# Two of six low parts a head from PSUM on VectorE, and the operand splits moved to GpSimd and ScalarE

## The chip, the cores and the metric

The kernel runs on one core of one Trainium2 chip. The metric is the device time of one execution in microseconds. A core has a tensor engine (PE, with its weight loads as PEld), a vector engine (DVE), a scalar engine (ACT), a GpSimd engine (POOL), and a sync engine (SP) that issues the transfers. The first three reach PSUM; GpSimd and the transfers work on SBUF.

## The reference

The inputs are q, k and v of 4 batches x 8 heads x 768 tokens x 64 columns. Queries and keys are given the nearest of 16 centroids of their head, and a query sees only the keys of its own cluster:

```python
q_assign = np.argmax(np.einsum('bhsd,hcd->bhsc', q_n, c_n), axis=-1)
k_assign = np.argmax(np.einsum('bhsd,hcd->bhsc', k_n, c_n), axis=-1)
mask = q_assign[:, :, :, None] == k_assign[:, :, None, :]
scores = np.where(mask, scale * np.matmul(q, k.transpose(0, 1, 3, 2)), -1e9)
scores = scores - np.max(scores, axis=-1, keepdims=True)
attn = np.exp(scores)
attn = attn / (np.sum(attn, axis=-1, keepdims=True) + 1e-09)
x = np.matmul(attn, v)          # then [3072, 512]: heads side by side
# soft mixture of experts on x: 8 experts, 4 slots each, 512 -> 1024 -> 512
logits = x @ phi
d = softmax(logits, axis=0); slot_input = d.T @ x
h = np.maximum(slot_input[e] @ w1[e], 0.0); slot_out[e] = h @ w2[e]
out = softmax(logits, axis=1) @ slot_out
```

The two softmax lines are shortened; all else is as in the reference.

## The kernel before

**What is done for a head.** There are 32 heads (a head here is one of 4 x 8), handled in pairs. Matrix products keep near float32 precision by splitting operands into a high and a low part. For each head `load_r` brings q and k, transposed, as one tile of 128 rows x 768 columns. `split_hi` rounds it (L512), `split_lo` takes the rest (L515), and ten small transfers (`place1`, `place2`, `place_mask`, `place3`, L325) lay the parts out as the operands of the score passes. For each pair, VectorE finds the cluster of each token (`assign1` to `assign3`, L473 to L488), and the mask goes into the operands too. V is split likewise into float16 parts (`splitv_hi`, L543, and `splitv_lo`, L547).

`pass_a` (L560) makes the scores of a head in nine steps of one PSUM bank each, with two banks in turn, and VectorE takes the row maxima of each step (`rowmax`, L568). The maxima are transposed and placed as one more operand row. `pass_b` (L603) then makes the scores again, less the maxima, with 128 keys on the partitions and 768 queries in the columns: six tiles a head, in two PSUM buffers `pb` in turn, an even tile in the first and an odd one in the second. ScalarE takes the exponential of a tile twice (`expo`, L609), once to float32 and once to float16, both in SBUF. The float16 copy is the high part; `elow` (L613) subtracts it from the float32 copy, on GpSimd, and writes the low part. `pass_c` (L625) multiplies both parts with the parts of v, two tiles at a time, and `norm` (L637 to L639) divides by the row sums.

**After the heads** the logits of each pair are added up, each batch of eight heads is routed, and at the end the experts' two layers run on 32 slots and the result is combined for all tokens (from L1022). Expert weights come in 16 chunks of 2 MB, five of them during the attention, the others into the buffers that the attention gives back.

**What sets the order.** Every step is recorded as an operation with an engine, an assumed duration and the buffers that it reads and writes. `Plan.order` goes through them with a clock of its own: each engine takes, of the operations that can start now or within the waiting time of their kind, the one with the lowest priority. Priorities are the numbers of the table `K`. The result is one fixed sequence for each engine, and on the chip an engine works through its sequence strictly in order, waiting on semaphores. The planner before assumes 0.23 us from one engine to another and knows nothing of one engine slowing another. `HI_ACT` is true for the heads 0 and 1 only, so from head 2 on both splits of q and k and both of v are VectorE's, while GpSimd does nothing but the six subtractions a head (in the last head two of six).

Of the kernel before, what the change touches and what calls it, by code (L numbers as in the profile page):

```python
# [21 lines left out]
HI_ACT = lambda i: i < 2 or i % 2 == HA  # L22
HA = 2
MX_ACT = False
WARM0 = 60
WARM1 = (0, 4, 3, 2, 4, 1)   # after the last xtrans, xtrans, logits, dtrans, slotin, comb
EARLY = 2              # heads whose first steps keep off the vector engine


class Plan:  # L30
    """Operations in program order, with the buffers that they read and write; order() lets every
    engine take, of the operations that can start or do so soon, the one of the lowest priority number."""

# [13 lines left out]
    def op(self, eng, us, key, t, fn, rd=(), wr=(), get=None, put=None, after=(), xfer=0.0):  # L47
# [16 lines left out]
        self.ops.append((eng, us, t + self.K[key], fn, deps, get, put, xfer, key, t))  # L64
# [12 lines left out]
    def order(self, look=LOOK, banks=1):  # L77
        N = len(self.ops)
        users = [[] for _ in range(N)]
        wait = [len(o[4]) for o in self.ops]  # L80
        for n, o in enumerate(self.ops):
            for d in o[4]:
                users[d].append(n)
        ready = [0.0] * N
        end = [None] * N
        free, cand, out = {}, {}, []
        dma = tail = 0.0
        gets, puts = [], {}

        def opened(n):  # L90
            cand.setdefault(self.ops[n][0], []).append(n)

        def start(n):
            t = ready[n]
            if self.ops[n][5] is not None and len(gets) >= banks:
                p = puts.get(gets[-banks])
                if p is None:
                    return None
                t = max(t, p + self.LAT)
            return t  # L100

        for n in range(N):
            if wait[n] == 0:
                opened(n)
        while len(out) < N:
            best = None
            for e, ns in cand.items():
                f = free.get(e, 0.0)
                ts = [(max(f, s), n) for s, n in ((start(n), n) for n in ns) if s is not None]
                if not ts:  # L110
                    continue
                t0 = min(ts)[0]
                if best is None or t0 < best[0]:
                    best = (t0, e, ts)
            t0, e, ts = best
            _, _, t, n = min((self.ops[n][2], n, t, n) for t, n in ts
                             if t <= t0 + self.K.get(self.ops[n][8] + "_wt", look))
# [14 lines left out]
            if get is not None:  # L132
                gets.append(get)
# [1099 lines left out]
```

## Time and profile before

| | |
|---|---|
| three runs | 564.26, 564.88, 568.58 us |
| median | 564.88 us |
| span of the profiled execution, first to last instruction | 563.4 us |
| busy: PE, DVE, ACT, POOL | 478.6, 465.5, 340.2, 345.7 us |
| normalisation of head 0, head 3, head 27, head 31 begins | 49.08, 107.45, 458.86, 498.95 us |

The profiled execution has no time of its own beside its span; the span is 0.9 us under the fastest of the three runs and 1.5 us under their median. The run has three stretches. Up to about 107 us the first heads fill the pipeline. From there to about 459 us the heads follow one another evenly. Then the last four heads run without preparation of further ones, and from about 499 us the experts follow.

A busy time includes what an instruction waits once it has started. On PE it also includes the modelled end of pipelined products, so that PE is never quite as busy as its figure. Two instructions that follow each other directly on VectorE overlap by about 0.08 us in the records.

### The profile page before, as it was taken

To read this page: it belongs to the slowest core of one execution; us is meant where nothing else is said; L and a number is where in the kernel's file an instruction comes from. 1 tells how busy PE (TensorE), PEld (TensorE's weight loads), DVE (VectorE), ACT (ScalarE), POOL (GpSimd) and SP (SyncE) were. 2 spreads that over 40 slices of the span, in tenths; PEclk is the share of its full clock that TensorE was granted. 3 is DMA by queue.
4 is the path that set the end of the run, shared out by engine and by line. 5 is a ranking of instruction groups with operands and counts; after the bars stand their busy time and mean duration, and the time that the engine had idled before them with its cause. 6 is when DMAs were issued, how large, how long until landed. Compare 5 with 4: busy or idle time off the path is not lost.

```text
span 563.4 us, 15227 instructions
## 1 busy us (share of the span) xinstructions
PE 478.6 (85%) x6083; PEld 376.8 (67%) x6083; DVE 465.5 (83%) x786; ACT 340.2 (60%) x494; POOL 345.7 (61%) x255
## 2 busy tenths in 40 slices
PE   8896868789888889789888889887988799899994
PEld 6685657577767667667676667776765678764484
DVE  3799698998989998989899998999899988452253
ACT  4176536676667667667676667676765687830142
POOL 7067465777767657777766578676866598714210
PEclk9999878999999999999999999999999899999998
DMA  8824537346656566676666646665765478999978
GB/s 222 216 70 120 152 98 204 102 130 186 172 142 178 147 154 164 178 177 155 169 168 180 155 125 161 181 176 151 174 175 151 132 204 203 308 311 382 408 248 239
DMA packets 55082, 103.79 MB, mean 184 GB/s; under 512 B 8490, under 2 KB 22372, under 8 KB 55012
## 3 DMA queue, kind: packets, MB, share of 16 engines
q1 hardware_dynamic: 55012, 102.82, 65.2%
q8 instruction: 48, 0.79, 0.6%
q14 instruction: 22, 0.18, 0.1%
HBM read 52.76 MB, written 6.29 MB: 105 GB/s over the span
## 4 chain that ended last, share of the span: by engine, by line
DVE 49%; PE 28%; DMA 12%; issue 5%; SPq 3%; ACT 1%; POOL 0%; DVEq 0%; ACTq 0%; POOLq 0%
DVE mc L568 16%; DMA w<-w 11%; DVE w L515 8%; PE pa L560 6%; PE pc L625 6%; DVE vx L543 5%; PE pb L603 5%; DVE w L512 3%; PE pso L1103 3%; PE ph L1041 2%; SPq L325 2%; DVE w L478 2%; DVE w L488 2%; DVE vx L547 2%; PE po L1124 2%
## 5 line engine op out<-in xcount | busy, mean ns | idle before, releaser
L613 POOL TENSOR_TENSOR w<-w,w 128x768 f16<-128x768 f32 x188 | 322.6, 1737 | 161.1 <-PE pc L625 81.7
L609 ACT ACTIVATE w<-pb 128x768 f32<-128x768 f32 (+1 forms) x384 | 285.0, 815 | 105.0 <-PE pb L603 102.5
L568 DVE TENSOR_REDUCE mc<-pa 128x1 f32<-128x512 f32 (+1 forms) x288 | 187.4, 679 | 17.9 <-PE pa L560 16.7
L560 PE MATMUL pa<-w 128*128 128x512 f32 (+1 forms) x384 | 120.9, 386 | 56.3 <-DVE mc L568 44.1
L603 PE MATMUL pb<-w 128*128 128x512 f32 (+1 forms) x576 | 152.6, 353 | 1.5 <-DMA w<-w 1.4
L625 PE MATMUL pc<-vx,w 128*128 128x65 f16 (+1 forms) x3456 | 123.0, 194 | 3.3 <-DVE w L639 3.0
L560 PEld LDWEIGHTS pa<-w 128*128 128x128 f32 x384 | 61.4, 191 | 89.0 <-DVE mc L568 72.4
L625 PEld LDWEIGHTS <-w 128*128 128x128 f16 x3456 | 112.3, 98 | 11.3 <-DVE w L639 3.9
L603 PEld LDWEIGHTS pb<-w 128*128 128x128 f32 x576 | 105.0, 193 | 18.2 <-issue 1.7
L603 PE MATMUL pb<-w,w 128*128 128x512 f32 x192 | 61.0, 340 | 0.0
L515 DVE TENSOR_TENSOR w<-w,w 128x768 fp32r<-128x768 f32 x30 | 48.9, 1630 | 0.1
L603 PEld LDWEIGHTS pb<-w,w 128*128 128x128 f32 x192 | 36.5, 190 | 7.1 <-DVE w L592 0.3
L543 DVE TENSOR_SCALAR vx<-w 128x384 f16<-128x384 f32 x30 | 35.6, 1185 | 0.0
L512 DVE CAST w<-w 128x768 fp32r<-128x768 f32 x30 | 27.6, 919 | 3.5 <-DMA w<-w 2.8
L462 ACT ACTIVATE w<-pt,crn 128x384 f32<-128x384 f32 x16 | 9.3, 581 | 30.7 <-PE pt L454 30.6
L547 DVE SCALAR_TENSOR_TENSOR vx<-w,vx 128x384 f16<-128x384 f32 x32 | 25.5, 797 | 1.8 <-ACT vx L541 1.7
L992 PE MATMUL pc<-ident 128*128 128x128 f32 x148 | 22.0, 301 | 1.4 <-POOL ident masks.py:199 1.4
L992 PEld LDWEIGHTS pc<-ident 128*128 128x128 f32 x148 | 20.2, 212 | 3.1 <-issue 1.6
L500 ACT ACTIVATE w<-pt,ohsc 128x768 fp32r<-128x768 bf16 x15 | 13.5, 901 | 12.5 <-PE pt L497 12.4
L653 ACT COPY xT<-pt 128x384 f32<-128x384 f32 x30 | 14.6, 488 | 10.0 <-PE pt L648 10.0
L488 DVE TENSOR_TENSOR w<-w,m 128x192 bf16<-128x192 bf16 x32 | 19.4, 645 | 0.3
L478 DVE TENSOR_TENSOR w<-w,descb 128x384 bf16<-128x384 bf16 x16 | 19.0, 1190 | 0.0
(138 smaller groups left out, 379.3 us busy)
## 6 DMA issues: line engine op xcount, KB each, us to landing
w<-w SPq DMA_DIRECT2D x128, 192.0 KB
w<-w SPq DMA_DIRECT2D x188, 96.0 KB
w<-w1r SPq DMA_DIRECT2D x64, 256.0 KB
w<-qkT SPq DMA_DIRECT2D x32, 384.0 KB
w<-w2a SPq DMA_DIRECT2D x32, 256.0 KB
w<-w2b SPq DMA_DIRECT2D x16, 512.0 KB
w<-vt SPq DMA_DIRECT2D x32, 192.0 KB
out<-w SPq DMA_DIRECT2D x24, 256.0 KB
```

Source lines behind the costliest of these rows:

```text
L488: nc.vector.tensor_tensor(oh[:, :, k, 0:NCL], wv[:, :, k, :], mv[:, :, k].unsqueeze(2).to_broadcast([P, NG // 2, NCL]), op=cmp)
L512: (nc.scalar.copy if HI_ACT(i) else nc.vector.tensor_copy)(RH[i % 2], R[i % 3])
L515: (nc.gpsimd if i < EARLY else nc.vector).tensor_sub(RL[i % 2], R[i % 3], RH[i % 2].bitcast(F32))
L543: nc.vector.tensor_scalar_mul(o, V[i % 2], VS)
L547: nc.vector.scalar_tensor_tensor(vx[:, :, 0:D], V[i % 2], VS, vx[:, :, D:2 * D], op0=ALU.mult, op1=ALU.subtract)
L560: nc.tensor.matmul(pa[:, c0:c0 + w], q1[:, q0:q0 + P], k1[:, k0:k0 + w], start=True, stop=True)
L568: nc.vector.tensor_reduce(hd[i]["mc"][:, 4 * m + c0:4 * m + c1], pa.rearrange("p (n c) -> p n c", n=c1 - c0), axis=AX.X, op=ALU.max, negat ...
L603: nc.tensor.matmul(pbt[j % 2][:, q0:q1], k_[:, kc], q_[:, q0:q1], start=(o == 0), stop=(o == 1))
L609: nc.scalar.activation(dst[:, j % 2, :], pbt[j % 2][:, 0:S], AF.Exp, scale=SCALE)
L613: eng.tensor_tensor(EL[(NT * i + j) % NEL], E32[o % 2][:, j % 2, :], EH[o % (NEH // 2)][:, j % 2, :], op=ALU.subtract)
L625: nc.tensor.matmul(pc[:, t * W:t * W + w], e[:, ts], vx[:, j, r0:r0 + w], start=(j == 0 and t == 0 and o == 0), stop=(j == NT - 1 and o == ...
L992: nc.tensor.matmul(d["pc"][:, 0:P], ident, ident, start=True, stop=True)
```

## The change

**Exponentials.** Of the six tiles of a head, the tiles 1 and 3 (`'PDPDPP'`; in the last head 1, 3 and 5) are handled in a new way. ScalarE still takes the exponential twice, now the float16 one first, and the float32 one is written over the scores in the `pb` buffer. VectorE subtracts from there (L607 of the changed kernel), and `pb` is free for the next scores only when it is done. The other four tiles are subtracted on GpSimd as before. The four float32 buffers in SBUF are now handed out to GpSimd's tiles alone, one by one.

**Splits.** From head 2 on, `split_hi` is ScalarE's in even heads and GpSimd's in odd ones, `split_lo` and `splitv_hi` are GpSimd's, and `splitv_lo` stays on VectorE. The heads 0 and 1 are as before.

**Constants.** The small constants of the last stage (`consts3`, `consts4`) are made at the start instead of in pair 1.

**Planner.** It lets an operation that it marks with `port`, and every operation of GpSimd, run only when no other such one does. Its latencies now differ by engine, transfers take longer in it, many durations are new, and the whole table `K` is new. The expert stage is the same.

```diff
-HI_ACT = lambda i: i < 2 or i % 2 == HA
-HA = 2
-MX_ACT = False
+SPLITS = (('ACT', 'POOL', 'POOL', 'DVE'), ('POOL', 'POOL', 'POOL', 'DVE'))
+EARLY_SPLITS = ("ACT", "POOL", "ACT", "DVE")
+LOWS = ('PDPDPP', 'PDPDPP')
+LAST_LOWS = "PDPDPD"
...
-    LAT = 0.23            # from one engine to another
-    DMA_ISSUE, DMA_DONE = 0.65, 1.0
+    LAT = {"PE": 0.22, "ACT": 0.22, "DVE": 0.14, "POOL": 0.14, "-": 0.0}
+    SAME = {"DVE": 0.11}
+    DMA_ISSUE, DMA_DONE = 1.25, 2.4
...
+            if o[10]:
+                t = max(t, port)
+            return max(t, free[o[0]])
...
+            if lock:
+                port = end
...
-    E32 = [cols(ar5, n * 2 * S, 2 * S).rearrange("p (t s) -> p t s", t=2) for n in range(2)]
+    NE32 = 4
+    E32 = [cols(ar5, n * S, S) for n in range(NE32)]
...
-        b3=-150.8, b4=97.0, b5=70.0, x=387.35, el=-51.8, c0=-14.95, c1=102.4, c2=224.45, c3=204.0,
+        maxrow_out=-367.85, b0=955.45, b1=175, b2=-738.8, b3=626.95, b4=-23.65, b5=335.4, x=322.8, el=-141.85,
...
+    ENG = dict(ACT=nc.scalar, DVE=nc.vector, POOL=nc.gpsimd)
+
+    def splits(i):
+        return EARLY_SPLITS if i < EARLY else SPLITS[i % 2]
+
+    def lows(i):
+        return LAST_LOWS if i == NH - 1 else LOWS[i % 2]
+
     def split_hi(i):
-        (nc.scalar.copy if HI_ACT(i) else nc.vector.tensor_copy)(RH[i % 2], R[i % 3])
+        e = splits(i)[0]
+        (nc.scalar.copy if e == "ACT" else ENG[e].tensor_copy)(RH[i % 2], R[i % 3])
 
     def split_lo(i):
-        (nc.gpsimd if i < EARLY else nc.vector).tensor_sub(RL[i % 2], R[i % 3], RH[i % 2].bitcast(F32))
+        ENG[splits(i)[1]].tensor_sub(RL[i % 2], R[i % 3], RH[i % 2].bitcast(F32))
...
     def splitv_hi(i):
-        o = VXs[i % 2][:, :, D:2 * D]
-        if i < EARLY:
-            nc.scalar.mul(o, V[i % 2], VS)
-        else:
-            nc.vector.tensor_scalar_mul(o, V[i % 2], VS)
+        e = splits(i)[2]
+        (nc.scalar.mul if e == "ACT" else ENG[e].tensor_scalar_mul)(VXs[i % 2][:, :, D:2 * D], V[i % 2], VS)
...
+    def e32(i, j):
+        if lows(i)[j] == "D":
+            return pbt[j % 2][:, 0:S]
+        return E32[e32n[NT * i + j] % NE32]
+
     def expo(i, j):
-        o = (NT * i + j) // 2
-        for dst in (E32[o % 2], EH[o % (NEH // 2)]):
-            nc.scalar.activation(dst[:, j % 2, :], pbt[j % 2][:, 0:S], AF.Exp, scale=SCALE)
-
-    def elow(i, j, eng):
-        o = (NT * i + j) // 2
-        eng.tensor_tensor(EL[(NT * i + j) % NEL], E32[o % 2][:, j % 2, :], EH[o % (NEH // 2)][:, j % 2, :],
-                          op=ALU.subtract)
+        n = NT * i + j
+        for dst in (EH[n // 2 % (NEH // 2)][:, j % 2, :], e32(i, j)):
+            nc.scalar.activation(dst, pbt[j % 2][:, 0:S], AF.Exp, scale=SCALE)
+
+    def elow(i, j):
+        n = NT * i + j
+        (nc.vector if lows(i)[j] == "D" else nc.gpsimd).tensor_tensor(
+            EL[n % NEL], e32(i, j), EH[n // 2 % (NEH // 2)][:, j % 2, :], op=ALU.subtract)
...
+    op("POOL", 0.6, "const1", 0, consts3, [], [("const", 3)])
+    op("DVE", 1.1, "const1", 0, consts4, [], [("const", 4)])
...
+                if lows(i)[j] == "D":
+                    op("ACT", 1.385, "x", t, lambda i=i, j=j: expo(i, j), [("pb", n)], [("eh", n), ("pb", n)])
+                    op("DVE", 0.88, "el", t, lambda i=i, j=j: elow(i, j), [("pb", n), ("eh", n)], [("el", n)])
```

**The order on VectorE**, in the evenly running stretch, behind the division of a head's result (`w_98` is the result, `w_97` a row of maxima or a part of an exponential, `w_88` and `w_89` the tile of q and k and its parts, `w_96` the tile of v, `vx` its parts, `pa` and `pb` the score banks). Before:

```order
L639 TENSOR_TENSOR w_98<-pc,z 128x2x3x64
L583 CAST w_97<-pt 6x128
L568 TENSOR_REDUCE mc<-pa_134 128x2
L568 TENSOR_REDUCE mc<-pa_133 128x1
L512 CAST w_89<-w_88 128x768
L543 TENSOR_SCALAR vx_121<-w_96 128x6x64
L568 TENSOR_REDUCE mc<-pa_134 128x1
L568 TENSOR_REDUCE mc<-pa_133 128x1
L515 TENSOR_TENSOR w_89<-w_88,w_89 128x768
```

and now, from the transfer of the maxima on:

```order
L571 CAST w_97<-pt 6x128
L535 SCALAR_TENSOR_TENSOR vx_121<-w_96,vx_121 128x6x64
L556 TENSOR_REDUCE mc<-pa_133 128x1
L607 TENSOR_TENSOR w_97<-pb_132,w_97 128x768
L556 TENSOR_REDUCE mc<-pa_133 128x1
L556 TENSOR_REDUCE mc<-pa_134 128x2
L453 TENSOR_REDUCE mx<-pt 128x24
L454 TENSOR_TENSOR w_88<-pt,mx 128x384
```

The three splits between the row maxima are gone, and a subtraction from the second score buffer (`pb_132`) stands there instead. A little later in the same pair the next one stands behind the products of the assignment:

```order
L556 TENSOR_REDUCE mc<-pa_134 128x2
L458 TENSOR_TENSOR w_88<-w_88,descb 128x384
L463 TENSOR_REDUCE m_3236<-w_88 128x24
L607 TENSOR_TENSOR w_97<-pb_132,w_97 128x768
L556 TENSOR_REDUCE mc<-pa_133 128x1
```

From here on the program repeats itself pair by pair: 41 instructions of VectorE, four of them subtractions, of which the other two stand right behind a row maximum.

**The order on GpSimd.** Before, 173 subtractions follow one another with nothing between them:

```order
L515 TENSOR_TENSOR w_89<-w_88,w_89 128x768 x2
L613 TENSOR_TENSOR w_97<-w_96,w_97 128x768 x15
L219 MEMSET grp 128x4
L221 MEMSET grp 32x1 x4
L613 TENSOR_TENSOR w_97<-w_96,w_97 128x768 x173
```

and now one pair of heads reads:

```order
L506 TENSOR_TENSOR w_89<-w_88,w_89 128x768
L607 TENSOR_TENSOR w_97<-w_96,w_97 128x768 x3
L531 TENSOR_SCALAR vx_121<-w_96 128x6x64
L607 TENSOR_TENSOR w_97<-w_96,w_97 128x768 x2
L503 CAST w_89<-w_88 128x768
```

The splits stand between subtractions that wait for ScalarE and for free buffers, and behind them on the queue.

## Rows read from the trace of the kernel before

**Rows 1.** Page, part 1: busy time, share of the span, instructions of each engine.

```profile
PE 478.6 (85%) x6083; PEld 376.8 (67%) x6083; DVE 465.5 (83%) x786; ACT 340.2 (60%) x494; POOL 345.7 (61%) x255
```

**Rows 2.** Windows: us, busy (count) of PE, PEld, DVE, ACT, POOL; PEclk, DMA.

```profile
100.00:400.00 300.00, 254.78 (x3338) 204.73 (x3337) 279.22 (x462) 204.29 (x293) 211.70 (x123) 1.00 0.61 159
```

**Rows 3.** Timeline (start us, us): divisions of heads 0, 3, 27, 31.

```profile
49.08 0.56 DVE L639 TENSOR_TENSOR w<-pc,z 128x384 f32<-128x384 f32 x1
...
107.45 0.56 DVE L639 TENSOR_TENSOR w<-pc,z 128x384 f32<-128x384 f32 x1
...
458.86 0.56 DVE L639 TENSOR_TENSOR w<-pc,z 128x384 f32<-128x384 f32 x1
...
498.95 0.36 DVE L639 TENSOR_TENSOR w<-pc,z 128x192 f32<-128x192 f32 x1
```

**Rows 4.** Waits from 100 to 400 us: us in total, times, longest us.

```profile
ACT w L609 <- PE pb L603: 68.7, 67, 2.4
...
POOL w L613 <- PE pc L625: 58.4, 29, 3.9
...
PE pa L560 <- DVE mc L568: 27.0, 34, 1.5
```

**Rows 5.** Page, part 4: the chain that ended last, by engine.

```profile
DVE 49%; PE 28%; DMA 12%; issue 5%; SPq 3%; ACT 1%; POOL 0%; DVEq 0%; ACTq 0%; POOLq 0%
```

**Rows 6.** Groups on VectorE: busy us, mean ns | idle before.

```profile
L515 DVE TENSOR_TENSOR w<-w,w 128x768 fp32r<-128x768 f32 x30 | 48.9, 1630 | 0.1
...
L543 DVE TENSOR_SCALAR vx<-w 128x384 f16<-128x384 f32 x30 | 35.6, 1185 | 0.0
...
L512 DVE CAST w<-w 128x768 fp32r<-128x768 f32 x30 | 27.6, 919 | 3.5 <-DMA w<-w 2.8 <-issue 0.7
...
L547 DVE SCALAR_TENSOR_TENSOR vx<-w,vx 128x384 f16<-128x384 f32 x32 | 25.5, 797 | 1.8 <-ACT vx L541 1.7
...
L478 DVE TENSOR_TENSOR w<-w,descb 128x384 bf16<-128x384 bf16 x16 | 19.0, 1190 | 0.0
```

**Rows 7.** Timeline, GpSimd and VectorE side by side, 267 to 273 us.

```profile
268.33 3.42 POOL L613 TENSOR_TENSOR w<-w,w 128x768 f16<-128x768 f32 x2 [0.22 <-PE pc L625]
...
267.39 1.14 DVE L512 CAST w<-w 128x768 fp32r<-128x768 f32 x1
...
268.45 1.80 DVE L543 TENSOR_SCALAR vx<-w 128x384 f16<-128x384 f32 x1
...
270.77 1.79 DVE L515 TENSOR_TENSOR w<-w,w 128x768 fp32r<-128x768 f32 x1
```

**Rows 8.** Lines on VectorE: ns min/median/max, first and last start.

```profile
L515 DVE TENSOR_TENSOR w<-w,w x30: 940/1796/2410, 21.7 to 462.3; 128x768 fp32r<-128x768 f32 x30
...
L543 DVE TENSOR_SCALAR vx<-w x30: 348/1264/1807, 52.7 to 482.4; 128x384 f16<-128x384 f32 x30
```

**Rows 9.** One line on VectorE with an operand in PSUM: min/median/max.

```profile
L639 DVE TENSOR_TENSOR w<-pc,z x33: 357/558/559, 49.1 to 499.6; 128x384 f32<-128x384 f32 x31, 128x192 f32<-128x192 f32 x2
```

**Rows 10.** Lines on GpSimd: duration ns min/median/max.

```profile
L613 POOL TENSOR_TENSOR w<-w,w x188: 1639/1654/2371, 33.6 to 494.1; 128x768 f16<-128x768 f32 x188
...
L515 POOL TENSOR_TENSOR w<-w,w x2: 1812/1816/1819, 7.3 to 9.1; 128x768 fp32r<-128x768 f32 x2
...
L321 POOL MEMSET w<- x4: 729/729/730, 2.2 to 5.8; 32x768 f32 x4
```

**Rows 11.** A line on ScalarE that heads 0 and 1 have: min/median/max.

```profile
L512 ACT CAST w<-w x2: 832/832/832, 5.4 to 7.3; 128x768 fp32r<-128x768 f32 x2
```

**Rows 12.** Copies of constants on VectorE: ns min/median/max, first and last start.

```profile
L225 DVE COPY stk<-ident x4: 1291/1582/1594, 72.3 to 76.8; 32x32 f32<-32x32 f32 x4
...
L226 DVE COPY w<-stk x1: 1606/1606/1606, 78.4 to 78.4; 128x128 f32<-128x128 f32 x1
```

**Rows 13.** Timeline, PE and ScalarE: one score tile and its exponentials.

```profile
275.59 0.39 PE L603 MATMUL pb<-w 128*128 128x512 f32 x1
...
276.56 1.51 ACT L609 ACTIVATE w<-pb 128x768 f32<-128x768 f32 x2 [1.44 <-PE pb L603]
```

More of the change, by code (lines that the diff above doesn't have):

```diff
@@ L45, in touching, with op @@
         return [o for t in tokens for o in self.touch.get(t, [])]
[L47 removed]
+    def op(self, eng, us, key, t, fn, rd=(), wr=(), get=None, put=None, after=(), xfer=0.0, port=False):
         n = len(self.ops)
@@ L75, in lead_tail, with order @@
             dict(logits=0.085, sims=0.085, onehot=0.054, disp=0.085, comb=0.085).get(key, 0.02)
-    def order(self, look=LOOK, banks=1):
-        N = len(self.ops)
+    def order(self, look=LOOK):
+        ops = self.ops
+        N = len(ops)
         users = [[] for _ in range(N)]
-        wait = [len(o[4]) for o in self.ops]
-        for n, o in enumerate(self.ops):
+        wait = [len(o[4]) for o in ops]
+        for n, o in enumerate(ops):
             for d in o[4]:
@@ L84, in order @@
         ready = [0.0] * N
[L85 to L91, printed above, removed]
+        free = {e: 0.0 for e in ("SP", "PE", "ACT", "DVE", "POOL", "-")}
+        cand = {e: [n for n in range(N) if wait[n] == 0 and ops[n][0] == e] for e in free}
+        out = []
+        dma = tail = port = 0.0
+        bank, bank_free = None, 0.0
         def start(n):
+            o = ops[n]
@@ L94, in start @@
             t = ready[n]
-            if self.ops[n][5] is not None and len(gets) >= banks:
-                p = puts.get(gets[-banks])
-                if p is None:
-                    return None
[L99 to L104, printed above, removed]
+            if o[5] is not None:
+                if bank is not None:
+                    return None
+                t = max(t, bank_free)
+            if o[10]:
+                t = max(t, port)
@@ L118, in order @@
-            eng, us, _, fn, _, get, put, xfer = self.ops[n][:8]
-            if eng == "PE":
-                lead, nt = self.lead_tail(self.ops[n][8])
+            for e in free:
+                ts = [(s, n) for s, n in ((start(n), n) for n in cand[e]) if s is not None]
+                if ts:
+                    t0 = min(ts)[0]
+                    if best is None or t0 < best[0]:
+                        best = (t0, e, ts)
+            t0, e, ts = best
+            _, n, t = min((ops[n][2], n, t) for t, n in ts if t <= t0 + self.K.get(ops[n][8] + "_wt", look))
@@ L821, in clustered_attention_then_soft_moe @@
             head = i
-            early = i < EARLY
-            op(*(("ACT", 0.75) if HI_ACT(i) else ("DVE", 0.47)), "split_hi", h0, lambda i=i: split_hi(i), [("R", i)], [("rh", i)])
+            sp = splits(i)
+            op(sp[0], dict(ACT=0.75, DVE=0.47, POOL=0.8)[sp[0]], "split_hi", h0, lambda i=i: split_hi(i), [("R", i)], [("rh", i)], port=True)
             for k in range(3):
-                op("SP", 0.625, "place1", h0, lambda i=i, k=k: place1(i, k), [("rh", i)], [("q1", i)], xfer=0.55)
```

281 lines of the change are left out of this document (124 added, 157 removed).

## The prediction

> **What bounds the kernel now.** I read the busy times first [rows 1]. PE has 85% and VectorE 83%, which decides nothing, since a busy PE holds the modelled ends of pipelined products. So I took a stretch in which the heads run evenly, 100 to 400 us [rows 2]: VectorE is busy for 279.22 of 300 us, PE for 254.78, GpSimd for 211.70, ScalarE for 204.29, all at a granted clock of 1.00. The timeline gives the pace [rows 3]: the division of head 3 begins at 107.45 us and that of head 27 at 458.86, so 24 heads take 351.41 us, or 14.64 us each. One head has then 14.64 x 279.22 / 300 = 13.63 us of VectorE, 12.43 of PE, 10.33 of GpSimd and 9.97 of ScalarE. VectorE idles for 1.01 us a head. The waits agree [rows 4]: PE waits 27.0 us for row maxima to free a score bank, ScalarE waits 68.7 us for scores, and the chain that ended last runs through VectorE for 49% of the span and through PE for 28% [rows 5]. VectorE sets the pace; PE is the next, 1.2 us a head below it.
>
> Why is VectorE so full? The reader should compare the means [rows 6] with the fastest instructions of the same lines [rows 8]. `split_lo` takes 1630 ns in the mean and 940 at best, `splitv_hi` 1185 and 348. The timeline shows the cause [rows 7]. GpSimd does two subtractions from 268.33 us, 3.42 us together. `splitv_hi` begins at 268.45 and ends at 270.25, when the first of them is about done; `split_lo` begins at 270.77 and ends at 272.56, some 0.8 us after the second. Such instructions stand still while GpSimd holds something that both need, and the record counts that as busy.
>
> **The change, part by part, for one head of the even stretch.**
>
> *Splits that leave VectorE.* The three means add up to 1.630 + 1.185 + 0.919 = 3.73 us [rows 6]. Neighbours overlap by 0.08 us in the records (`split_hi` at 267.39 ends at 268.53, and `splitv_hi` begins at 268.45 [rows 7]), so 3.49 us of VectorE's time are freed.
>
> *Two subtractions from PSUM.* No row shows this instruction. The nearest is the division, also two tensors, one of them in PSUM [rows 9]: 357 ns for 192 columns and 558 for 384, so 201 ns for 192 more, and 558 + 402 = 960 ns for 768. Its largest is 559 ns beside a median of 558, so it never stood still for GpSimd. The ends: 0.94 us, the fastest `split_lo`, and 1.80 us, its median, if the subtraction had to wait like it [rows 8]. I take 0.96, since the division is the form with an operand in PSUM. Two are 1.92 us, less 0.16 of overlap 1.76. VectorE's net: 13.63 - 3.49 + 1.76 = **11.90 us**.
>
> *What GpSimd gets.* Two subtractions go: 2 x 1.65 = 3.31 us [rows 10]. `split_lo` comes with 1.82 us (same rows, from the early heads). For `splitv_hi` and `split_hi`, with one input, the rows give a memset of 768 columns as the low end, 0.73 us, and the two-input 1.82 as the high one: 0.36 to 0.91 us for 384 columns, 0.73 to 1.82 for 768 in every second head. I take 0.5 and 0.8, near the memset, as one stream is read. GpSimd: 10.33 - 3.31 + 1.82 + 0.5 + 0.4 = 9.74 us, at most 10.66. That is below VectorE, so it costs nothing unless it delays somebody (rivals). The page "GPSIMD Engine Reference" of the Trainium skill, section "Elementwise — side-by-side cycle accounting", gives one-input bodies 1.03 cycles an element; at its 1.2 GHz I estimate 0.66 us for 768 columns and 0.33 for 384 before dispatch, with which GpSimd would have 9.5 us; no row here shows such an instruction.
>
> *What ScalarE gets.* `split_hi` of the even heads, 832 ns [rows 11], so 0.42 us a head: 10.39 us, hidden under VectorE and PE. That its second exponential goes to PSUM I cost at nothing: it may be shorter or longer than the 0.8 us it takes now, and ScalarE has over 2 us a head to spare.
>
> *Constants.* Four copies of about 1.58 us and one of 1.61 leave VectorE at 72.3 to 80.0 us [rows 12], 7.6 us in all. At the start they stand before any row maximum. Bounds 0 and 7.6; I take 6, since at 72 us VectorE has other work waiting.
>
> *The even stretch.* VectorE's load falls by 1.73 us a head, but the pace does not fall by as much: PE's 12.43 us is now the larger load, though an upper figure, and VectorE's is close beneath it. Two engines that wait for each other through two score banks leave more gaps than one that leads. If PE's gaps closed, 12.5 us would be left; if under half of the load's fall came through, 14.0. I take 13.2, which keeps VectorE at 90% (now 93%) and PE at 94% of its modelled load.
>
> *Sum.* Even stretch: 24 x (14.64 - 13.2) = 34.6 us. Heads 1 to 3 (49.08 to 107.45 us): 3 x 1.44 = 4.3, and 6 for the constants. The last four heads take 40.1 us, 10.0 each [rows 3], already under VectorE's load of a full head, so it is not what limits them; 1 us for one subtraction fewer on VectorE. The experts: nothing. Together 46 us: 563.4 - 46 = 517.4 us of span. The median of the runs stands 1.5 us above the span, so **519 us**. Bounds: 12.5 a head gives 51.4 + 6.4 + 7.6 + 1 = 66, or 499; 14.0 with nothing for the constants gives 15.4 + 1.9 + 0 = 17, or 548.
>
> **The rivals.**
>
> *Slower: the score buffer is held too long.* Tiles 1 and 3 keep the second `pb` buffer until VectorE has subtracted, and VectorE takes its work in a fixed order. One tile's scores begin at 275.59 us, its exponentials at 276.56 and take 1.51 us [rows 13]. A tile of the new kind holds the buffer 0.97 + 1.51 + 0.96 and about 0.2 for two handovers, 3.64 us plus its wait w on VectorE; tile 5 holds it 2.6. A head needs 9.9 + 2w. This passes 14.64 at w = 2.4 us. For it: ahead of a subtraction stand a row maximum (about 0.6) or a product of the assignment, which itself waits for GpSimd (1190 ns in the mean, rows 6). While the buffer is held PE can't begin the next tile, and the row maxima behind it are late too. Against: in the printed order three of four stand behind one row maximum. At w = 2.8 a head takes 15.5 us: 27 x 0.86 = 23 slower, 6 for the constants: 582 us. Chance 0.09.
>
> *No change: the standing still moves instead of going.* What still has two operands in SBUF on VectorE (`splitv_lo` 797 ns, a product of the assignment 1190, rows 6) takes up what the splits waited, 0.69 + 0.84 us and more a head; or the new subtraction waits for GpSimd like `split_lo`, so that the change doesn't do what it says, 2 x 0.84 us. Either takes the 1.73 us back: 563.4 - 6 + 1.5 = 559 us. The page "Perfetto Trace Analysis" of the Trainium skill, section "Optimizing Scalar/DVE Operations", says that moving work between VectorE and GpSimd might not help, since they share a read port; by that rule this would be the outcome. The division's steady 558 ns speaks against it, and two subtractions leave GpSimd for what three splits bring. Chance 0.07.
>
> *Half of it: splits come late.* On GpSimd a split stands behind up to three subtractions, 5 us, and these wait for buffers that the products free (58.4 us in 300 now, rows 4). Behind a split stand ten transfers on SP's queue, the score passes of the next head, and loads that need the buffer. With 13.9 us a head: 24 x 0.74 + 2 + 6 = 26, so 539 us. Chance 0.18.
>
> *Better: the remaining standing still goes too.* Then VectorE is near 11 us and PE sets 12.5 a head: 499 us. Chance 0.16.
>
> **How the numbers follow.** The forecast, 507 to 531 us, has 0.50. Faster by over 1% (5.6 us, about what a measurement of this kernel tells from no change) holds it, the half and the better case: 0.84. Within 1%: 0.07. Slower: 0.09. A range from 497 to 548 us takes in the bounds, most of the better case and of the half; about 2 in 10 lie outside.
>
> **What would show it.** Of the changed kernel: the subtraction on VectorE at 0.94 to 1.0 us with a maximum close to its median; VectorE's busy time down by some 50 us over the span; 13 to 13.5 us from one head's division to the next; `split_lo` on GpSimd near 1.8 us and the one-input splits under 1 us. PE's waits for row maxima should shrink. I am wrong if PE waits long for VectorE before scores into the second buffer (the slower rival), if VectorE's remaining two-operand lines grow (no change), or if PE waits for transfers behind GpSimd's splits (half).

## The result, and the profile after

The changed kernel takes **530.28 us** (median of four runs, 527.71 to 531.66) beside 564.57 us for the kernel before on the same chip: a ratio of **0.943 [0.937, 0.949]**. The forecast was 519 us, 497 to 548. The time lies in that range, 11 us above the forecast, and the gain did not come from where the forecast had put it.

The page after, busy time by engine as in [rows 1], and the chain that ended last, as in [rows 5]:

```profile
PE 474.6 (90%) x6083; PEld 373.5 (71%) x6083; DVE 429.2 (81%) x757; ACT 347.0 (66%) x509; POOL 337.7 (64%) x269
...
PE 41%; DVE 22%; issue 13%; POOL 10%; DMA 5%; ACT 4%; SPq 2%; POOLq 0%; ACTq 0%; DVEq 0%
```

VectorE lost 36 us of busy time, not 50. The chain runs through it for 22% of the span, after 49%, and PE leads with 41%. The timeline shows the divisions of heads 0, 3, 27 and 31 (start in us, duration), to hold against [rows 3]:

```profile
48.08 0.56 DVE L633 TENSOR_TENSOR w<-pc,z 128x384 f32<-128x384 f32 x1
...
82.97 0.56 DVE L633 TENSOR_TENSOR w<-pc,z 128x384 f32<-128x384 f32 x1
...
421.25 0.56 DVE L633 TENSOR_TENSOR w<-pc,z 128x384 f32<-128x384 f32 x1
...
462.93 0.36 DVE L633 TENSOR_TENSOR w<-pc,z 128x192 f32<-128x192 f32 x1
```

| stretch | before, us | after, us | difference | forecast |
|---|---|---|---|---|
| to head 0 | 49.08 | 48.08 | -1.0 | 0 |
| heads 1 to 3 | 58.37 | 34.89 | **-23.5** | -10.3 |
| heads 4 to 27 | 351.41 (14.64 a head) | 338.28 (14.10) | **-13.1** | -34.6 |
| heads 28 to 31 | 40.09 | 41.68 | +1.6 | -1 |
| experts | 64.45 | 64.27 | -0.2 | 0 |
| span | 563.4 | 527.2 | -36.2 | -46 |

The profiled executions of two kernels below, the constants moved in the old order and the new splits in the old order, took 566 us each, above their medians; times of single stretches from them are rough. There are two questions: why the even stretch gave 0.54 us a head and not 1.44, and why the first heads gave twice what was forecast.

The even stretch by windows (us, then busy time and count of PE, PEld, DVE, ACT, POOL; granted clock, DMA), to hold against [rows 2]:

```profile
100.00:400.00 300.00, 269.24 (x3520) 213.87 (x3523) 275.68 (x465) 215.94 (x315) 214.02 (x138) 1.00 0.64 170
```

By the working of the prediction, VectorE has now 14.10 x 275.68 / 300 = 12.96 us a head (13.63 before, 11.90 forecast). Its lines in that window (count, busy us, mean ns, idle before):

```profile
L607 DVE TENSOR_TENSOR w<-pb,w 128x768 f16<-128x768 f32 x43 | 40.9, 951 | 1.5 <-ACT pb L603 0.9
L535 DVE SCALAR_TENSOR_TENSOR vx<-w,vx 128x384 f16<-128x384 f32 x21 | 35.7, 1699 | 0.5
L470 DVE TENSOR_TENSOR w<-w,m 128x192 bf16<-128x192 bf16 x20 | 17.4, 912 | 0.0
L458 DVE TENSOR_TENSOR w<-w,descb 128x384 bf16<-128x384 bf16 x10 | 12.5, 1255 | 0.0
```

The same lines of the kernel before in the same window, with the splits that left:

```profile
L515 DVE TENSOR_TENSOR w<-w,w 128x768 fp32r<-128x768 f32 x20 | 36.8, 1842 | 0.0
L543 DVE TENSOR_SCALAR vx<-w 128x384 f16<-128x384 f32 x21 | 26.6, 1265 | 0.0
L512 DVE CAST w<-w 128x768 fp32r<-128x768 f32 x21 | 20.8, 990 | 2.3 <-DMA w<-w 1.6 <-issue 0.7
L547 DVE SCALAR_TENSOR_TENSOR vx<-w,vx 128x384 f16<-128x384 f32 x20 | 15.3, 765 | 0.0
L478 DVE TENSOR_TENSOR w<-w,descb 128x384 bf16<-128x384 bf16 x10 | 12.2, 1223 | 0.0
...
L488 DVE TENSOR_TENSOR w<-w,m 128x192 bf16<-128x192 bf16 x20 | 11.2, 597 | 0.1
```

The three lines that stay (V's low part, the two products of the assignment) took 0.77 + 0.60 + 0.61 = 1.97 us a head, the last at half a time a head, and take 1.70 + 0.91 + 0.63 = 3.24 now. That is 1.27 us of standing still which moved from the splits to them. The balance of a head is then: splits 1.84 + 1.27 + 0.99 less 0.24 of overlap = -3.86; subtractions 2 x 0.95 less 0.16 = +1.74; standing still +1.27; together -0.85, against -0.67 by the windows. The first two terms were forecast nearly so (-3.49, +1.76). The third was put wholly into a rival.

The timeline shows V's low part standing still, with GpSimd beside it:

```profile
307.22 1.17 POOL L531 TENSOR_SCALAR vx<-w 128x384 f16<-128x384 f32 x1 [1.72 <-PE pc L619]
308.36 3.58 POOL L607 TENSOR_TENSOR w<-w,w 128x768 f16<-128x768 f32 x2
...
308.09 0.27 DVE L571 CAST w<-pt 6x128 fp32r<-6x128 f32 x1
308.43 2.00 DVE L535 SCALAR_TENSOR_TENSOR vx<-w,vx 128x384 f16<-128x384 f32 x1
```

`splitv_lo` needs what `splitv_hi` writes, so it can't begin before GpSimd ends L531 at 308.39 us. At that moment GpSimd begins its next instruction, a subtraction, and L535 ends at 310.43, just after the first of the two subtractions (308.36 + 3.58 / 2 = 310.15). Eight of its 21 instructions in the stretch begin like this, within 0.05 us of the end of `splitv_hi`, and take 1.99 to 2.00 us. Eight others begin over 4 us after that end, but 0.3 to 0.4 us into a `split_lo` of GpSimd, the other split that moved there, and take 1.85 to 1.91 us:

```profile
325.94 1.83 POOL L506 TENSOR_TENSOR w<-w,w 128x768 fp32r<-128x768 f32 x1 [2.39 <-ACT w L503]
...
326.30 1.88 DVE L535 SCALAR_TENSOR_TENSOR vx<-w,vx 128x384 f16<-128x384 f32 x1
```

Of the other five, the three that begin while GpSimd does nothing take 0.54 or 0.55 us. Durations over the whole run (min/median/max in ns) show how common the standing still is, and the subtraction from PSUM as free of it:

```profile
L535 DVE SCALAR_TENSOR_TENSOR vx<-w,vx x32: 538/1859/2003, 13.3 to 447.7; 128x384 f16<-128x384 f32 x32
...
L607 DVE TENSOR_TENSOR w<-pb,w x65: 934/950/958, 30.8 to 460.8; 128x768 f16<-128x768 f32 x65
...
L531 POOL TENSOR_SCALAR vx<-w x30: 1173/1174/1255, 47.1 to 444.5; 128x384 f16<-128x384 f32 x30
L503 POOL CAST w<-w x15: 817/822/827, 33.7 to 425.2; 128x768 fp32r<-128x768 f32 x15
L506 POOL TENSOR_TENSOR w<-w,w x32: 1814/1827/1843, 7.4 to 426.1; 128x768 fp32r<-128x768 f32 x32
```

In the kernel before, V's low part had a median of 550 ns:

```profile
L547 DVE SCALAR_TENSOR_TENSOR vx<-w,vx x32: 543/550/1880, 11.0 to 483.5; 128x384 f16<-128x384 f32 x32
```

From head 2 on both of V's splits stood on VectorE there, and 15 of the 20 low parts in the stretch began while GpSimd did nothing. Last, the waits of the stretch (us in total, times, longest), as in [rows 4]:

```profile
ACT w L603 <- PE pb L591: 64.7, 49, 3.3
POOL vx L531 <- PE pc L619: 52.3, 21, 4.4
...
PE pa L548 <- DVE mc L556: 13.9, 16, 1.3
...
PE pb L591 <- DVE w L607: 4.0, 7, 0.7
```

PE waits half as long for row maxima (13.9 us, 27.0 before), and for VectorE to free a score buffer 4.0 us only. GpSimd stands for 52.3 us at `splitv_hi`, whose buffer the products of an earlier head still read.

### The profile page after: what moved, and what is told of

Same layout as the page of the kernel before. It is cut to its first block, busy times and chain, and to the rows that moved or that the text cites. A ratio compares the mean times of both kernels' runs of the same rounds, so it can differ in the third digit from the quotient of the medians.

```text
span 527.2 us, 15330 instructions
## 1 busy us (share of the span) xinstructions
PE 474.6 (90%) x6083; PEld 373.5 (71%) x6083; DVE 429.2 (81%) x757; ACT 347.0 (66%) x509; POOL 337.7 (64%) x269
## 4 chain that ended last, share of the span: by engine, by line
PE 41%; DVE 22%; issue 13%; POOL 10%; DMA 5%; ACT 4%; SPq 2%; POOLq 0%; ACTq 0%; DVEq 0%
PE pb L591 11%; POOL w L607 8%; DVE mc L556 7%; PE pc L619 7%; PE pa L548 6%; DMA w<-w 5%; DVE w L607 4%; DVE vx L535 4%; PE pc L990 3%; PE pso L1101 3%; ACT w L603 3%; PE ph L1039 3%; DVE w L470 2%; POOL vx L531 2%; SPq L335 2%
## 5 line engine op out<-in xcount | busy, mean ns | idle before, releaser
L603 ACT ACTIVATE w<-pb 128x768 f16<-128x768 f32 (+1 forms) x319 | 240.2, 816 | 87.5 <-PE pb L591 85.0
L607 POOL TENSOR_TENSOR w<-w,w 128x768 f16<-128x768 f32 x127 | 215.1, 1710 | 25.6 <-ACT w L603 19.5
L591 PE MATMUL pb<-w 128*128 128x512 f32 (+1 forms) x576 | 158.5, 360 | 8.3 <-DVE w L607 6.1
L548 PE MATMUL pa<-w 128*128 128x256 f32 (+1 forms) x384 | 112.4, 369 | 21.8 <-DVE mc L556 17.3
L506 POOL TENSOR_TENSOR w<-w,w 128x768 fp32r<-128x768 f32 x32 | 58.5, 1828 | 40.2 <-ACT w L503 27.1
L531 POOL TENSOR_SCALAR vx<-w 128x384 f16<-128x384 f32 x30 | 35.3, 1177 | 61.8 <-PE pc L619 61.8
L607 DVE TENSOR_TENSOR w<-pb,w 128x768 f16<-128x768 f32 x65 | 61.9, 952 | 14.7 <-ACT pb L603 12.3
L603 ACT ACTIVATE pb<-pb 128x768 f32<-128x768 f32 x65 | 53.7, 826 | 0.0
L535 DVE SCALAR_TENSOR_TENSOR vx<-w,vx 128x384 f16<-128x384 f32 x32 | 43.3, 1354 | 1.0 <-POOL vx L531 0.5
L591 PEld LDWEIGHTS pb<-w,w 128*128 128x128 f32 x192 | 36.2, 189 | 4.8
L633 DVE TENSOR_TENSOR w<-pc,z 128x384 f32<-128x384 f32 (+1 forms) x33 | 18.0, 546 | 1.1
```

Source lines behind the costliest of these rows:

```text
L506: ENG[splits(i)[1]].tensor_sub(RL[i % 2], R[i % 3], RH[i % 2].bitcast(F32))
L531: (nc.scalar.mul if e == "ACT" else ENG[e].tensor_scalar_mul)(VXs[i % 2][:, :, D:2 * D], V[i % 2], VS)
L535: ENG[splits(i)[3]].scalar_tensor_tensor(vx[:, :, 0:D], V[i % 2], VS, vx[:, :, D:2 * D], op0=ALU.mult, op1=ALU.subtract)
L548: nc.tensor.matmul(pa[:, c0:c0 + w], q1[:, q0:q0 + P], k1[:, k0:k0 + w], start=True, stop=True)
L591: nc.tensor.matmul(pbt[j % 2][:, q0:q1], k_[:, kc], q_[:, q0:q1], start=(o == 0), stop=(o == 1))
L603: nc.scalar.activation(dst, pbt[j % 2][:, 0:S], AF.Exp, scale=SCALE)
```

## The experiments

The theory after this reading: the work that left VectorE is what pays, and the even stretch gave little because V's low part stands still, behind `splitv_hi` or beside `split_lo`, both now on GpSimd. Rivals: the subtractions hold the score buffer; the constants or the new order of the plan, not the new engines, made the gain. Ratios are to the kernel before. "Pace" is the time a head between the divisions of heads 3 and 27. The fixed sequences stay as they are unless a line says that the plan was made anew.

### The constants alone

Kernel before, `consts3` and `consts4` recorded at the start, so the plan was made anew:

```diff
+    op("POOL", 0.6, "const1", 0, consts3, [], [("const", 3)])
+    op("DVE", 1.1, "const1", 0, consts4, [], [("const", 4)])
...
-            op("POOL", 1.0, "const2", 0, consts3, [("xn", 0)], [("const", 3)])
-            op("DVE", 1.4, "const2", 0, consts4, [("const", 3)], [("const", 4)])
```

> The kernel before, with only the constants of the last stage made at the start instead of in pair 1; its planner and priorities are the old ones. Theory: of the 23.5 us that heads 1 to 3 gained, the constants are 6 to 7.6, because at 72 to 80 us VectorE had row maxima waiting: 557 to 559 us, and head 3 divides at about 100 instead of 107.5 us. Rival: the copies stood in time that was free anyway, and all of the early gain is the new order: 563 to 566 us.

Measured: 567.64 us, ratio 1.005 [1.000, 1.010], pace 15.00. No gain: heads 1 to 3 take 48.6 us in its profile, 9.8 less than before, and the even stretch (15.00 a head, 14.64 before) and the last four heads (46.4 us, 40.1 before) give it back in the plan's other order. So the sequences of the kernel before were kept and only the calls moved ahead of them (the two operations stay in the plan and issue nothing):

```diff
+    consts3()
+    consts4()
...
-            op("POOL", 1.0, "const2", 0, consts3, [("xn", 0)], [("const", 3)])
+            op("POOL", 1.0, "const2", 0, lambda: None, [("xn", 0)], [("const", 3)])
```

(and the same for the other). 

> The kernel before in its old order, with nothing changed but that the constants are made at the start; the earlier run of the same idea let the planner find a new order, whose even stretch was 0.36 us a head slower. Theory: head 3 divides 6 to 11 us earlier, and with the even stretch unchanged at 14.6 us a head that stays to the end: 554 to 559 us. Rival: the even stretch waits for something that the early heads don't decide, and takes it back: 562 to 566 us.

Measured: 561.21 us, 0.994 [0.990, 0.999]: about 3 us, half of the 6 forecast. What the constants did is seen in windows of the kernel before:

```profile
70.00:75.00 5.00, 5.00 (x89) 4.48 (x87) 4.99 (x7) 3.56 (x5) 4.75 (x8) 1.00 0.46 118
75.00:80.00 5.00, 0.15 (x5) 0.02 (x1) 4.94 (x5) 0.88 (x2) 4.91 (x4) 0.77 0.41 104
80.00:85.00 5.00, 4.35 (x29) 3.68 (x30) 4.91 (x9) 1.58 (x3) 0.00 (x0) 0.55 0.34 96
```

VectorE is busy for 4.94 of 5 us, with the copies of [rows 12]; PE does 0.15 us of work, and the mean granted clock falls from 1.00 (2.4 GHz) to 0.77 and then 0.55, which is nearly all at 1.2 GHz. With the constants moved in the old order PE has 4.08, 4.40 and 2.29 us in these windows, at a clock of 1.00 throughout. After the change the same three windows have PE at 4.55, 5.00 and 4.46 us and a clock of 1.00 throughout.

### New engines in the old order, old engines in the new order

Old order with the splits' engines of the change (all six low parts stay on GpSimd):

```diff
+SPLITS = (('ACT', 'POOL', 'POOL', 'DVE'), ('POOL', 'POOL', 'POOL', 'DVE'))
...
-        (nc.gpsimd if i < EARLY else nc.vector).tensor_sub(RL[i % 2], R[i % 3], RH[i % 2].bitcast(F32))
+        ENG[run_splits(i)[1]].tensor_sub(RL[i % 2], R[i % 3], RH[i % 2].bitcast(F32))
```

> The kernel before in its old order, instruction by instruction, with only the engines of the splits exchanged as in the change (from head 2 on split_hi on ScalarE or GpSimd, split_lo and splitv_hi on GpSimd); all six subtractions a head stay on GpSimd, which then has 10.3 + 3.4 = 13.7 us a head. Theory: VectorE loses 3.5 us a head and gets some standing still back, so VectorE no longer sets the pace but GpSimd does, at 14 us or more a head: 555 to 580 us, GpSimd over 90% busy in the even stretch. Rival (the placement of the splits is what pays, the rest is little): below 545 us.

Measured: 559.76 us, 0.987 [0.977, 0.997]; in its profile VectorE's load is 2.7 us a head below that of the kernel before and the pace no better, 14.81. GpSimd has 13.4 us a head there, and V's low part, median 1385 ns, stands still in the old order as well.

New order with all four splits on VectorE from head 2 on, the subtractions as changed:

```diff
+RUN_SPLITS = (('DVE', 'DVE', 'DVE', 'DVE'), ('DVE', 'DVE', 'DVE', 'DVE'))
...
-        e = splits(i)[0]
+        e = run_splits(i)[0]
```

(likewise for the other three.) 

> The changed kernel in its own order, with the splits of q, k and v back on VectorE from head 0 on; VectorE still subtracts two tiles a head from the score buffer. Theory (VectorE's load, with what it stands still, sets the pace, plus about 1.2 us a head): the splits add 1.6 us a head at their fastest and one to two more in standing still, so VectorE has 14.5 to 15.5 us and a head takes 15.7 to 16.7: 568 to 592 us. Rival (the new order is what pays, the engines of the splits little): 545 us or less.

Measured: 602.68 us, 1.062 [1.049, 1.076], pace 16.72: 72 us slower than the changed kernel and above the expected range. VectorE has 16.72 x 274.62 / 300 = 15.31 us a head there, as expected.

The same, and in heads 2 to 27 all six low parts on GpSimd too, so that the engines are those of the kernel before:

> The changed kernel in its own order with the old engines: splits on VectorE, and in heads 2 to 27 all low parts on GpSimd from SBUF. What is left of the change is the order, the constants at the start and the last four heads. Theory (the engines are what pays; the order is made for other engines): no faster than the kernel before, 560 to 585 us. Rival (the order pays by itself): 550 us or less, above all with head 3 dividing before 95 us instead of 107.5.

Measured: 595.99 us, 1.060 [1.053, 1.067], pace 16.19, above the expected range too. The new order is worse than the old for the old engines, and the old order gains 1.3% with the new splits, by an interval that ends just under 1. Only together do they give 6%. In both kernels of the new order with old splits PE's granted clock is 0.95 to 0.96 in the even stretch, 1.00 in the change; how much of their loss is due to that was not separated.

### The subtraction from PSUM taken back

New order, new engines of the splits, but in heads 2 to 27 all six low parts on GpSimd from SBUF:

```diff
     def e32(i, j):
+        if 2 <= i < 28:
+            return E32[(NT * i + j) % NE32]
...
-        (nc.vector if lows(i)[j] == "D" else nc.gpsimd).tensor_tensor(
+        (nc.vector if lows(i)[j] == "D" and not 2 <= i < 28 else nc.gpsimd).tensor_tensor(
```

> The changed kernel in its own order; in heads 2 to 27 all six low parts are subtracted on GpSimd from SBUF, as before the change. Theory: VectorE loses 1.8 us a head, but GpSimd gets 3.4 and has 13.5 us a head, and sets a pace of 14.1 to 15: 530 to 552 us. Rival (the score buffer that VectorE holds limits the even stretch): the buffer is free earlier, and the time is 524 us or less.

Measured: 522.39 us, 0.929 [0.922, 0.936], pace 13.58. The interval lies just below that of the whole change. So what gives the change its name **costs** here some 8 us, 12 by the pace of the 24 heads. VectorE has 13.58 x 255.02 / 300 = 11.54 us a head there, and GpSimd is full. V's low part stands still as before, 1668 ns in the mean, and the pace is better all the same, which speaks for VectorE's load as a whole and not for that line alone; the score buffer is also free earlier here. The window, and behind it that line:

```profile
100.00:400.00 300.00, 277.42 (x3642) 222.29 (x3641) 255.02 (x438) 226.66 (x330) 298.98 (x190) 1.00 0.67 179
```

```profile
L535 DVE SCALAR_TENSOR_TENSOR vx<-w,vx 128x384 f16<-128x384 f32 x22 | 36.7, 1668 | 4.4 <-POOL vx L531 4.1
```

VectorE's two low parts again, but from the float32 exponential in SBUF, so that the score buffer isn't held:

```diff
-        if lows(i)[j] == "D":
-            return pbt[j % 2][:, 0:S]
-        return E32[e32n[NT * i + j] % NE32]
+        return E32[(NT * i + j) % NE32]
```

(In its last heads these buffers share their place with expert weights that have come in, so its last stretch computes on other values and its output is wrong.)

> The changed kernel in its own order; the two tiles a head that VectorE subtracts have their float32 exponential in one of the four SBUF buffers instead of in the score buffer, which is free again after the second exponential. Theory: with both operands in SBUF the subtraction stands still while GpSimd works, as split_lo did (median 1.80 us), so its mean goes from 0.95 to 1.3 to 1.8 us, VectorE's load rises by 0.7 to 1.7 us a head: 545 to 575 us. Rival: the score buffer, held until VectorE has subtracted, is what limits the even stretch, and freeing it earlier gains more: 515 to 525 us.

Measured: 524.78 us, 0.930 [0.924, 0.935], pace 13.32. The subtraction itself is slower, as its durations show:

```profile
L605 DVE TENSOR_TENSOR w<-w,w x65: 935/959/2475, 31.0 to 458.5; 128x768 f16<-128x768 f32 x65
```

935 ns at best as from PSUM, but up to 2475, mean 1.26 us in the even stretch: with both operands in SBUF it stands still at times. The Trainium skill, page "SBUF — State Buffer", section "Who interferes with whom", says that a VectorE instruction with two SBUF inputs contends with a GpSimd instruction that reads SBUF, and that one with at most one SBUF input doesn't, outside VectorE's 2-port modes. 934 to 958 ns from PSUM and 935 to 2475 from SBUF agree with it. `splitv_hi`, with its one input, stood still on VectorE too before the change [rows 8]; whether in such a mode, no run shows. The even stretch of this kernel is 338.3 - 319.8 = 18.5 us shorter than that of the change, and its last four heads lose 9 of them (50.7 us, 41.7 in the change). That it was faster all the same spoke for a cost of the held buffer; a later run, on another kernel, finds none.

### V's high part on ScalarE

The one that the theory asks for: `splitv_hi` leaves GpSimd, all else as changed.

```diff
+RUN_SPLITS = (('ACT', 'POOL', 'ACT', 'DVE'), ('POOL', 'POOL', 'ACT', 'DVE'))
```

> The changed kernel in its own order, with only splitv_hi on ScalarE (0.53 us) instead of GpSimd (1.18 us). Theory: splitv_lo on VectorE takes 1.55 us a head in the even stretch, 1.0 more than it needs, since splitv_hi ends on GpSimd, a subtraction follows there at once, and splitv_lo comes too late for what both need. With splitv_hi on ScalarE it should take 0.7 to 1.0 us in the mean, VectorE should lose 0.5 to 0.8 us a head, and the time falls to 515 to 524 us. Rival: PE's own load and its waits for score buffers set the pace now, and the time stays at 527 to 533 us although splitv_lo gets shorter.

Measured: **517.2 us, 0.915 [0.909, 0.921]**, pace 13.44, some 13 us faster than the change. The same lines between 100 and 400 us, and behind them that window:

```profile
L539 DVE SCALAR_TENSOR_TENSOR vx<-w,vx 128x384 f16<-128x384 f32 x23 | 16.8, 730 | 0.2 <-issue 0.2
L471 DVE TENSOR_TENSOR w<-w,m 128x192 bf16<-128x192 bf16 x22 | 15.6, 748 | 0.0
L459 DVE TENSOR_TENSOR w<-w,descb 128x384 bf16<-128x384 bf16 x11 | 14.1, 1280 | 0.0
L535 ACT ACTIVATE vx<-w 128x384 f16<-128x384 f32 x22 | 11.9, 541 | 2.0 <-PE pc L623 2.0
```

```profile
100.00:400.00 300.00, 282.20 (x3693) 225.51 (x3693) 265.47 (x488) 239.25 (x357) 194.24 (x122) 1.00 0.67 179
```

V's low part takes 730 ns, 1699 in the change (not the 1.55 us of the expectation), and the work on ScalarE takes 541 ns against 1177 on GpSimd. VectorE has 13.44 x 265.47 / 300 = 11.89 us a head, the very load that was forecast for the change (11.90), and the pace is 13.44 where 13.2 was forecast for it. GpSimd's wait of 52.3 us is gone too (2.0 us on ScalarE). How much of the 13 us is due to the one and how much to the other was not separated; in the run from SBUF GpSimd still waits 34.8 us at `splitv_hi`, at a pace of 13.32, which speaks against that wait alone.

### Both together

V's high part on ScalarE and, in heads 2 to 27, all low parts on GpSimd (the two edits above in one):

> The changed kernel's order; the high part of V is on ScalarE and in heads 2 to 27 all six low parts are taken on GpSimd from the float32 exponential in SBUF. Theory (the standing still of the low part of V and the subtraction from PSUM are two separate losses, and they add): -13 us and -8 us on 530, less what GpSimd's load of some 12.3 us a head against TensorE's 12.6 still costs, 503 to 512 us, 12.9 to 13.3 us a head between heads 3 and 27, the low part of V under 0.8 us. Rival (both runs met the same next bound, TensorE's own chain and the full queue of GpSimd): 514 to 521 us, 13.4 us a head or more.

Measured: 521.02 us, 0.923 [0.918, 0.927], pace 13.55. The theory that the two gains add fell. VectorE's load is down to 13.55 x 248.76 / 300 = 11.24 us and the pace does not follow. V's low part takes 1260 ns again, beside a GpSimd that is busy for 271.72 of 300 us:

```profile
100.00:400.00 300.00, 277.94 (x3645) 222.13 (x3643) 248.76 (x438) 238.29 (x355) 271.72 (x167) 1.00 0.69 179
```

The same kernel with VectorE reading one column of the score buffer where its subtraction stood, so that it holds the buffer at next to no cost:

```diff
+        if lows(i)[j] == "D" and 2 <= i < 28:
+            held = wk1.tile([P, 1], F32, name="held")
+            nc.vector.tensor_tensor(held, pbt[j % 2][:, 0:1], EH[n // 2 % (NEH // 2)][:, j % 2, 0:1], op=ALU.subtract)
```

> As the kernel with the high part of V on ScalarE and all lows on GpSimd, but in heads 2 to 27 VectorE still reads one column of the score buffer and of the high part of tiles 1 and 3, at the place in its order where its subtraction stood: the buffer is held until VectorE gets there, at some 0.1 to 0.4 us an instruction. Theory (the subtraction from PSUM loses because it holds the score buffer): 6 to 15 us slower than that kernel, 12.9 -> 13.3 us a head or more, and TensorE waits for VectorE at its second product. Rival (it loses by VectorE's time of 0.94 us and by where the work lands): within 4 us of that kernel.

Measured: 520.87 us, 0.924 [0.920, 0.928], pace 13.54. In the stretch the 44 reads take 151 ns each:

```profile
L617 DVE TENSOR_TENSOR held<-pb,w 128x1 f32<-128x1 f32 x44 | 6.7, 151 | 3.1 <-ACT w L609 2.9
```

The held buffer costs nothing there. VectorE has 11.49 us a head in that kernel and 12.96 in the change, so it may come to the buffer sooner than there.

V's high part on ScalarE and VectorE's low parts from SBUF in heads 2 to 27:

> The changed kernel's order; the high part of V is on ScalarE, and VectorE keeps its two low parts a head but in heads 2 to 27 reads the exponential from SBUF. Theory (the held buffer costs, and the low part of V no longer stands still): 508 to 515 us, about 13.0 us a head; VectorE's subtraction 1.0 to 1.3 us since two operands in SBUF can stand still beside GpSimd. Rival (the subtraction with two operands in SBUF takes over the standing still): 517 us or more, subtraction over 1.4 us.

Measured: 525.86 us, 0.933 [0.928, 0.938], pace 13.84, slower than from PSUM (0.915). The subtraction takes 1.11 us in the mean, V's low part 0.98, and now GpSimd's copy stands still too: 1306 ns, where it had 826 with the subtraction from PSUM.

```profile
L613 DVE TENSOR_TENSOR w<-w,w 128x768 f16<-128x768 f32 x43 | 47.7, 1110 | 2.4 <-ACT w L609 2.2
...
L507 POOL CAST w<-w 128x768 fp32r<-128x768 f32 x11 | 14.4, 1306 | 12.8 <-DMA w<-w1r 9.7 <-DMA w<-w 3.2
```

With V's high part on ScalarE, PSUM is the better place to read from. The four SBUF buffers also serve six tiles a head here instead of four; what that costs was not separated.

### The planner's rule on the port

The change without the two lines that let port users run one at a time in the plan; engines the same, plan made anew:

```diff
-            if o[10]:
-                t = max(t, port)
```

> The changed kernel with the planner's rule on the shared port left out (two lines: an instruction with two operands in SBUF no longer starts behind the other engine's in the plan), so the order differs and the engines are the same. Theory (the rule places VectorE's two-operand work where GpSimd leaves room): 535 to 550 us, two-operand lines of VectorE standing still 0.3 us a head or more longer. Rival (the order that the engines really keep is set by waits, not by the planned starts): within 5 us of 530.

Measured: 566.14 us, 1.004 [1.000, 1.008]: the whole gain is gone, more than expected. The mechanism expected is not what did it, as the lines and the window of the same stretch show:

```profile
L533 DVE SCALAR_TENSOR_TENSOR vx<-w,vx 128x384 f16<-128x384 f32 x20 | 31.4, 1572 | 3.6 <-POOL vx L529 2.7 <-DMA w<-w 0.8
L468 DVE TENSOR_TENSOR w<-w,m 128x192 bf16<-128x192 bf16 x20 | 12.2, 650 | 0.0
...
L456 DVE TENSOR_TENSOR w<-w,descb 128x384 bf16<-128x384 bf16 x11 | 7.3, 667 | 0.1
```

```profile
100.00:400.00 300.00, 270.47 (x3400) 213.26 (x3398) 251.92 (x444) 217.32 (x314) 209.08 (x136) 0.98 0.62 163
```

The three lines stand still **less** than in the change (1.57 + 0.65 + 0.33 = 2.56 us a head, 3.24 there), and VectorE is idle for 48 of 300 us. It waits 27.0 us for score passes, and head 0 ends at 58.8 us, not 48.1. In this plan the engines wait for each other, and PE, at a clock of 0.98, needs 13.3 us a head for the same work. The table `K` belongs to a plan with the rule. So the run shows that the sequence is worth 36 us, not that the chip's port is what made it so.

## Why the prediction was right, and where it was wrong

**Right in sum, by two errors that partly cancel.** That the time came out 11 us from the forecast is in part luck. The even stretch gave 21.5 us less than forecast, the first heads 13.2 more. With the small terms the span is 9.8 us longer than forecast, and the median stands 3.1 us above it, not 1.5.

**The subtraction from PSUM: right.** 0.96 us taken, 0.951 found, 934 to 958 over 65. The division with its steady 558 ns [rows 9] was the right neighbour. What it wins was wrong: beside the splits' new places it is no gain at all. VectorE was still the fuller engine, and 1.74 us a head went onto it. With V's high part on ScalarE it neither clearly gains nor costs: 0.915 [0.909, 0.921] with it, 0.923 [0.918, 0.927] without.

**The failed step: VectorE's load a head, 11.90 us.** The splits were costed with their standing still, and all of it was booked as freed. 1.27 us of it came back on the lines that stayed. The prediction had this as its "no change" rival (0.07), as all or nothing; it came as a part. The page "Perfetto Trace Analysis" of the Trainium skill, section "Optimizing Scalar/DVE Operations", had warned that work moved between the two might not help; here a third of 3.86 us was lost that way. With most of the standing still of V's low part gone (V's high part on ScalarE), the load came out at 11.89 and the pace at 13.44. The step from load to pace, 1.3 us on top, held in the change and in this kernel (1.14 and 1.55 us), but it is no rule: the subtraction from SBUF alone has 0.94 us on top, the new splits in the old order 3.85.

**GpSimd's splits.** `split_lo` 1.83 us as forecast, `split_hi` 0.82 (0.8 taken). `splitv_hi` 1.17 instead of 0.5, outside my ends of 0.36 to 0.91; per column it costs 3.1 ns against 1.1 for the copy. The estimate by the page "GPSIMD Engine Reference" of the Trainium skill, section "Elementwise — side-by-side cycle accounting" (0.33 us before dispatch), was further off still. GpSimd's load was not the point, 10.06 us a head; where `splitv_hi` stands was.

**Half (0.18): partly.** GpSimd does wait, 52.3 us at `splitv_hi`, but PE waits for transfers only 1.4 us in the stretch, so the splits don't delay the scores in the way described.

**The slower rival: wrong.** PE waits 4.0 us in 300 for VectorE to free a buffer, 0.7 at most, and holding it alone cost nothing in the kernel where that was tried.

**The first heads.** Heads 1 to 3 took: 58.4 us before; 52.5 with the constants moved, 50.4 with the new splits, both in the old order; 48.6 with only the constants moved and the plan made anew; 43.8 with the old engines in the new order, 40.0 with its splits on VectorE, 39.5 in the plan without the port rule; 34.9 in the change. The forecast of 6 us for the constants was of the right size here, since 58.4 - 52.5 = 5.9, though half of it was gone at the end of the run. What I left out is the new sequence: 58.4 - 43.8 = 14.6 us with the old engines, a part of it the constants; since head 0 comes 4.7 us later in that kernel, 9.9 us are left at head 3. I had read the table `K` as moving work, and given the plan no term of its own.

**What sets the next bound** is argued, not shown. The chain that ended last speaks for PE; with V's high part on ScalarE, beside 28% for PE and 49% for VectorE before [rows 5]:

```profile
PE 61%; DVE 13%; ACT 11%; issue 5%; DMA 5%; SPq 3%; POOL 1%; ACTq 0%; DVEq 0%; POOLq 0%
```

Four kernels with 11.2 to 11.9 us a head on VectorE have a pace of 13.44 to 13.58, PE has 12.5 to 12.6 us in each and is the fullest engine in three of them; in the other GpSimd is. The reading from SBUF at 12.4 us on VectorE and a pace of 13.32 doesn't fit a simple rule by loads; why it beat the change stays open, since the held buffer cost nothing where that was tried, in a kernel with V's high part on ScalarE.

## What to carry to other kernels

An instruction's time beside another engine holds two things, its own work and its standing still; moving it frees the first, and a part of the second may come back on instructions that stay. Here V's low part took it up: in 8 of 21 cases it waited for the other engine and so began just as that engine went on, in 8 it ran into a split that had moved there. Move work to an engine outside the conflict: one split on ScalarE was worth 13 us here. Moving producer and consumer together was not tried. And a change that comes with a new plan is two changes: cost the sequence by itself.

## What the runs showed of the hardware

`splitv_hi`, one input, 384 columns of float32 to float16 in six rows of 64, takes 1.17 us on GpSimd and 0.54 on ScalarE; a copy of 768 columns on GpSimd takes only 0.82. ScalarE's exponential takes 807 ns (median) to PSUM and 810 to SBUF, where float16 and float32 are counted together; the means to float32 are 826 and 816. PSUM gains nothing here, though the page "ScalarE: Activation LUTs" of the Trainium skill, section "Step-by-step: what each stage is for", calls PSUM the faster destination. The durations in the changed kernel:

```profile
L603 ACT ACTIVATE w<-pb x319: 790/810/897, 29.0 to 459.3; 128x768 f16<-128x768 f32 x117, 128x768 f32<-128x768 f32 x43
...
L603 ACT ACTIVATE pb<-pb x65: 806/807/900, 29.8 to 460.0; 128x768 f32<-128x768 f32 x65
```

The standing still goes both ways: GpSimd's copy went from 826 to 1306 ns in the mean beside VectorE's subtractions from SBUF.
